# First K transfer in two, two wo transfers in one, and one head's softmax earlier, in a cached-attention decode block

## The chip, the core and the metric

The kernel runs on one NeuronCore of one Trainium2 chip. The core has a matrix engine (PE, whose weight loads are shown as PEld), a vector engine (DVE), a scalar engine (ACT), a general engine (POOL), and a queue of its own, SyncE (SP), which here does nothing but issue transfers from HBM into the on-chip memory, SBUF. Sixteen DMA engines carry these transfers out. The metric is the device time of one execution in microseconds. The median of three runs of the kernel before is 355.0 us (354.94 to 355.05).

## The reference

One token passes through a decoder block. Cut to what matters:

```
mod = silu(c) @ w_mod                     -> six vectors of 512: sa, ca, ga, sb, cb, gb
h   = layernorm(x) * (1 + ca) + sa        x: 1 x 512
q   = h @ wq                              32 heads of 128
for each of 8 KV heads g (4 query heads share one):
    s = q_g . k_cache[g] / sqrt(128)      32768 positions x 128
    p = softmax(s);   o_g = p @ v_cache[g]
x   = x + ga * (concat(o) @ wo)           wo: 4096 x 512
h   = layernorm(x) * (1 + cb) + sb
x   = x + gb * (relu(h @ w1) @ w2)        w1: 512 x 1792, w2: 1792 x 512
```

All inputs are bf16. The two caches are 64 MB each; everything else adds some 13 MB. Every byte is read once, so the block moves 149.42 MB from HBM for very little arithmetic per byte.

## The kernel before, in words

**The stream.** All large inputs come through one list, `stream` (L139 to L144), whose entries are issued in order on the SP queue by `load` and `stream_dma`. A K or V entry is half a head: two "steps" of 64 cache rows per partition, 32 KB on each of the 128 partitions, 4 MB in all. The order is: first half of head 0's K, `w_mod`, `wq`, second half of head 0's K; then, for g from 0 to 6 and for each half, K of head g+1 and V of head g; then V of head 7 (one transfer of two steps, two of one step); then `wo` in four parts, which belong to heads 0 to 3, 4 and 5, 6, and 7 (`WOP`, L47); then `w1` in two parts and `w2` in six. Towards the end of the list the parts get smaller: the two last `wo` parts are 512 KB, the eight `w1` and `w2` parts 1344 to 128 KB.

**Slots and semaphores.** The destinations are five slots of 32 KB per partition (the pool `ring`), used in turn; several small parts share one slot (`piece`). SP can issue an entry only when the compute that read the slot's previous content has finished. The framework also gives the transfers eight completion semaphores in turn, so SP waits until the transfer eight places earlier has landed. When an entry can be issued, it queues behind the entries before it.

**The heads.** For each head, DVE first transposes a quarter of K in place (`turn_k`, L413, four 2.28 us instructions per half head), PE multiplies it with the queries (`scores`, L429), DVE copies the scores of a half head and takes their maximum (`bank_max`, L435). `softmax(g)` (L440) is a Python generator in six pieces, which are emitted one at a time between other work by `next(soft)`: the maximum over the halves (DVE, `m_p`); its transpose (PE, `mT_ps`); the maximum over rows and its spread (DVE, `Mrow`, `Mexp`); the transpose back and the exponential (PE `Mb_ps`, ACT `nbias`, `P_g`); the transpose of the probabilities and the row sums (DVE `PT_g`, `Lexp`); the sum over partitions (PE, `L_ps`); and, when the generator ends, its reciprocal (DVE, `Linv`). `pv(g, (u, u'))` (L484) multiplies the probabilities with half a V: for most heads a loop of the PE's own sequencer (L499), whose entry waits for what the loop needs; for the last stretch it is unrolled.

**The order.** The order of PE and DVE instructions is the one written in the main loop (L606 to L693, `manual_schedule`). Iteration g does the scores of head h = g+1 and, between them, the rest of head g's softmax, the sums of head g-1 (`blocks`, `o_cols`, `normalise`), and both V halves of head g.

**The tail.** After the last V, PE works through a fixed list: `project(0)` to `project(3)` multiply the heads' outputs with the four parts of `wo` (L568 for the first two, L574 for the last two, 16 matmuls with 16 weight loads each), with `join_rows` (L591) between them and a few matmuls without use (`keep_clock`, L604) that keep PE busy. Then come the residual and the second layernorm (L698 to L714, DVE, ACT and two short PE steps), the `w1` product (L721, 16 matmuls, 12 of which need the first `w1` part and the last 4 the second), a transpose and relu (L731, L732), the `w2` product (L742, 56 matmuls, 16 + 12 + 12 + 8 + 4 + 4 for the six parts), two DVE steps (L747, L749) and the store of the result.

Of the kernel before, what the change touches and what calls it, by code (L numbers as in the profile page):

```python
# [17 lines left out]
def kernel(  # L18
# [15 lines left out]
    P = 128  # L34
    _, _, D = A_x.shape
    _, Hkv, Sk, Dh = A_k_cache.shape
    Hq = A_wq.shape[1] // Dh
    REP = Hq // Hkv
# [4 lines left out]
    TK = 64  # L43
# [2 lines left out]

    WOP = [(0, Hkv // 2), (Hkv // 2, Hkv // 4), (Hkv - 2, 1), (Hkv - 1, 1)]  # L47
    WOROWS = 2
    LAST = Hkv - 1
    LOOPED = Hkv - 2  # L50
    W2P = [(0, 4), (4, 7), (7, 10), (10, 12), (12, 13), (13, 14)]
# [9 lines left out]
    vv = A_v_cache[0].rearrange("g (p j) d -> g p j d", p=P)  # L61
    wm_v = w_mod.rearrange("(p kt) n -> p kt n", p=P)
    wq_v = A_wq.rearrange("(p kt) n -> p kt n", p=P)
    def wo_v(i):
        g0, n = WOP[i]
        return A_wo[g0 * REP * Dh:(g0 + n) * REP * Dh, :].rearrange("(p r) d -> p r d", p=P)

    w1_v = B_w1.rearrange("(p kt) f -> p kt f", p=P)
    w2_v = B_w2.rearrange("(p f) d -> p f d", p=P)

# [15 lines left out]
    loaded, last_loop = {}, []  # L86
# [3 lines left out]
    def piece(name, at, n):  # L90

        if name not in pieces:
            pieces[name] = ring.tile([P, 2 * TK * Dh], BF16, tag="slot", name=name)
        return pieces[name][:, at:at + n]

    def load(key):
        kind = key[0]
        if kind == "wm":
            t = ring.tile([P, KT, 6 * D], BF16, tag="slot", name="wm_sb")
            src = wm_v  # L100
        elif kind == "wq":
            t = ring.tile([P, KT, Hq * Dh], BF16, tag="slot", name="wq_sb")
            src = wq_v
        elif kind in "kv":
            g, steps = key[1], key[2]
            src = (kv if kind == "k" else vv)[g, :, TK * steps[0]:TK * (steps[-1] + 1), :]
            name = "Ksb" if kind == "k" else "Vsb"
            if len(steps) == 2:
                t = ring.tile([P, TK * len(steps), Dh], BF16, tag="slot", name=name)
            else:  # L110
                t = piece(name, TK * Dh * (steps[0] % 2), TK * Dh).rearrange("p (j d) -> p j d", d=Dh)
        elif kind == "wo":
            g0, n = WOP[key[1]]
            t = piece("wo_sb", g0 * REP * D, n * REP * D).rearrange("p (r d) -> p r d", d=D)
            src = wo_v(key[1])
        elif kind == "w1":
            k0, k1 = W1P[key[1]]
            t = piece("w12_sb", k0 * Dff, (k1 - k0) * Dff).rearrange("p (kt f) -> p kt f", f=Dff)
            src = w1_v[:, k0:k1]
        else:  # L120
            f0, f1 = W2P[key[1]]
            t = piece("w12_sb", KT * Dff + f0 * D, (f1 - f0) * D).rearrange("p (f d) -> p f d", d=D)
            src = w2_v[:, f0:f1]
        stream_dma(t[:], src)
        if kind in "kv":
            for i, u in enumerate(steps):
                loaded[(kind, g, u)] = t[:, TK * i:TK * (i + 1), :]
        else:
            loaded[key] = t[:]

    def stream_dma(dst, src):
        i = nc.sync.dma_start(out=dst, in_=src)
        tc.stamp_issue_order_token(i.ins, "sp_stream")
        if last_loop:

            tc.add_manual_dep(i.ins, last_loop[0], mybir.DependencyInfo(
                mybir.DependencyClass.NoSync, mybir.DependencyReason.DATA))

    stream = [("k", 0, (0, 1)), ("wm",), ("wq",)] + [("k", 0, (2 * G, 2 * G + 1)) for G in range(1, NG)]  # L139
    for g in range(LAST):  # L140
        for G in range(NG):
            stream += [(kind, gg, (2 * G, 2 * G + 1)) for kind, gg in (("k", g + 1), ("v", g))]
    stream += [("v", LAST, (0, 1)), ("v", LAST, (2,)), ("v", LAST, (3,))] + [("wo", i) for i in range(len(WOP))]
    stream += [("w1", i) for i in range(len(W1P))] + [("w2", i) for i in range(len(W2P))]  # L144
    pos = [0]

# [22 lines left out]
    for hp in range(4):  # L169
        h, par = hp // 2, hp % 2  # L170
# [213 lines left out]
    def build_qbd(g):  # L384
        d_ap = qbd[g % 2][:]
        d_ps = d_ap.ap[0][0]
        s_ap = qrep_sb[:]
        s_ps = s_ap.ap[0][0]
        for a in range(4):
            o = AP(d_ap.tensor, d_ap.offset + (32 * a) * d_ps + 4 * 7 + 32 * a,  # L390
                   [[d_ps, 32], [QW, 4], [1, 4]])
            i = AP(s_ap.tensor, s_ap.offset + (32 * a) * s_ps + REP * g,
                   [[s_ps, 32], [Hq, 4], [1, 4]])
            nc.scalar.copy(out=o, in_=i)  # L394
# [8 lines left out]
    def turn_k(g, u, half):  # L403

        if u == 0 and half == 0:
            S_tiles[g] = spool.tile([P, NG, 512], F32, tag="S_g", name="S_g")
            m_tiles[g] = spool.tile([P, NG], F32, tag="m2", name="m2")
        Ksb = need(("k", g, u))
        KTt = Ksb[:, 32 * half:32 * half + 32, :].rearrange("p j d -> p (j d)")
        KT_tiles[g, u, half] = KTt  # L410
        if g == 0 and u < 2:
            return
        t = nc.vector.transpose(out=KTt.bitcast(F32), in_=KTt.bitcast(F32))  # L413
        if loop:

            tc.add_manual_dep(t.ins, loop.pop(), mybir.DependencyInfo(
                mybir.DependencyClass.NoSync, mybir.DependencyReason.DATA))
# [188 lines left out]
    with tc.manual_schedule(engines={mybir.EngineType.PE, mybir.EngineType.DVE}):  # L606
# [7 lines left out]
        soft = softmax(0)  # L614
# [2 lines left out]
        soft = None  # L617
        for g in range(LAST):
            h = g + 1
            build_qbd(h)  # L620
            turn_k(h, 0, 0)
            turn_k(h, 0, 1)
            turn_k(h, 1, 0)
            scores(h, 0, 0)
            if soft:
                next(soft)
            open_o(g)
            scores(h, 0, 1)
            if soft:
                next(soft)  # L630
            if g > 0:
                blocks(g - 1)
            scores(h, 1, 0)
            if g > 0:
                o_cols(g - 1)
            turn_k(h, 1, 1)
            scores(h, 1, 1)
            if soft:
                next(soft)
            if g > 0:  # L640
                normalise(g - 1)
                if g in [sum(w) for w in WOP]:
                    spread(part_of(g - 1))
            if soft:
                next(soft)
            bank_max(h, 0)
            next(soft or iter(()), None)
            pv(g, (0, 1))
            for u in (2, 3):
                for half in range(2):  # L650
                    turn_k(h, u, half)
                    scores(h, u, half)
            bank_max(h, 1)
            soft = softmax(h)
            next(soft)
            if g < LOOPED:
                pv(g, (2, 3))
                next(soft)
                continue
            next(soft)  # L660
            next(soft)
            pv(g, (2,), range(6))
            next(soft)
            next(soft)
            open_o(LAST)
            pv(g, (2,), range(6, 16))
            pv(g, (3,))
            next(soft)
            next(soft, None)
            a_rows.append(row_bank("a_ps"))  # L670
            blocks(g)
# [109 lines left out]
```

## Time and profile before

| | |
|---|---|
| median of three runs | 355.0 us |
| profiled execution, its own time | 355.01 us |
| its span, first to last instruction | 353.2 us |
| bytes read from HBM, mean rate over the span | 149.42 MB, 423 GB/s |
| share of the 16 DMA engines, SP's queue | 98.5% |
| PE busy | 281.2 us (80%), 1311 matmuls |
| DVE busy | 202.7 us (57%) |
| ACT busy, POOL busy | 25.5 us (7%), 3.9 us (1%) |
| mean granted PE clock | 0.951 |

The span is 1.8 us shorter than the execution's own time; what lies around it is start and end of the program. A share of a busy engine is an average over the whole span and says little about one stretch of it. A group's row gives the line and engine, the operation, what it writes and reads, the count, busy time and mean of one instruction, and then the idle time of that engine right before them and what ended it. The row of a transfer gives the queue, the count, the size, and the median time from issue to landing, which includes the time spent behind earlier transfers.

### The profile page before, as it was taken

The page shows a single profiled execution, that of the slowest core. Times are in us where ns is not written, and L with a number is a line of the kernel's source. Part 1 is how long each engine was busy: PE and PEld are TensorE (multiplying, and loading weights), DVE is VectorE, ACT ScalarE, POOL GpSimd, SP SyncE. Part 2 cuts the span into 40 slices and gives each one's busy share as a digit, 9 for nine tenths or more (in the row PEclk, how much of TensorE's full clock was granted, in tenths as well). Part 3 has the DMA queues.
Part 4 walks back from the last instruction along what each step waited for, and adds up shares of the span by engine and source line. Part 5 has one row for each costly group of instructions (what it writes and reads, how often), then busy time and mean ns, then how long its engine had stood idle before and what let it go on. Part 6 is the DMA issues. An engine that isn't in the chain of part 4 may idle for free. (4 is left out here: it accounts for less than half of the span.)

```text
span 353.2 us, 4005 instructions
## 1 busy us (share of the span) xinstructions
PE 281.2 (80%) x1311; PEld 112.2 (32%) x1311; DVE 202.7 (57%) x271; ACT 25.5 (7%) x69; POOL 3.9 (1%) x16
## 2 busy tenths in 40 slices
PE   0064865499798979897989799979689797989996
PEld 0021322133233333333333333323234233334444
DVE  6672074867458745872769177553938095743141
ACT  1200103000001000100010001000100000011000
POOL 4000000000000000000000000000000000000000
PEclk9995689589999999999999999999969999999999
DMA  8999999999999999999999999999999999999995
GB/s 356 405 426 449 437 416 438 449 419 419 455 430 416 449 442 416 417 460 427 419 453 432 416 442 439 428 414 449 442 416 445 438 423 417 453 434 410 424 419 203
DMA packets 6852, 149.59 MB, mean 423 GB/s; under 512 B 824, under 2 KB 1080, under 8 KB 1976
## 3 DMA queue, kind: packets, MB, share of 16 engines
q1 hardware_dynamic: 6776, 149.43, 98.5%
q8 instruction: 8, 0.13, 0.1%
q14 instruction: 4, 0.03, 0.0%
q0 software_dynamic: 64, 0.00, 0.0%
HBM read 149.42 MB, written 0.00 MB: 423 GB/s over the span
## 5 line engine op out<-in xcount | busy, mean ns | idle before, releaser
L413 DVE STREAM_TRANSPOSE Ksb<-Ksb 128x2048 f32<-128x2048 f32 x60 | 133.9, 2280 | 37.7 <-DMA Ksb<-in_A_k_cache_dram 37.7
L491 PE MATMUL o_ps<-Vsb,PT_g 128*16 (+1 forms) x512 | 128.1, 383 | 21.9 <-issue 9.9
L429 PE MATMUL S_ps<-Ksb,qbd 128*128 128x512 bf16 x512 | 124.0, 395 | 12.4 <-DVE Ksb L413 9.6
L429 PEld LDWEIGHTS <-qbd 128*128 128x128 bf16 x512 | 49.4, 99 | 78.1 <-issue 22.1
L491 PEld LDWEIGHTS o_ps<-Vsb,PT_g 128*16 x416 | 36.1, 87 | 90.2 <-issue 65.9
L435 DVE TENSOR_SCALAR_CACHE_REDUCE S_g<-S_ps 128x512 f32<-128x512 f32 x16 | 11.0, 690 | 52.9 <-PE S_ps L429 52.9
L394 ACT COPY qbd<-qrep_sb 32x16 bf16<-32x16 bf16 x32 | 6.4, 201 | 130.3 <-PE S_ps L429 129.2
L472 DVE STREAM_TRANSPOSE PT_g<-P_g 128x1024 bf16<-128x1024 bf16 x8 | 9.8, 1224 | 7.0 <-ACT P_g L466 7.0
L491 PEld LDWEIGHTS <-PT_g 128*16 128x16 bf16 x96 | 8.2, 90 | 11.0
L463 ACT ACTIVATE nbias<-Mb_ps 128x1 f32<-128x1 f32 x8 | 1.4, 171 | 133.4 <-PE Mb_ps L461 133.4
L295 PE MATMUL mod_ps<-wm_sb,siluT 128*1 128x512 bf16 x24 | 3.6, 624 | 7.4 <-DMA wm_sb<-in_w_mod_dram 7.4
L466 ACT ACTIVATE P_g<-S_g,nbias 128x1024 bf16<-128x1024 f32 x8 | 9.2, 1148 | 0.2
L227 PE MATMUL xc_ps<-cx_sel,cx_bd 16*128 16x2 bf16 x4 | 0.3, 172 | 11.2 <-DVE cx_bd L221 11.2
L358 DVE STREAM_TRANSPOSE Ksb<-Ksb 128x2048 f32<-128x2048 f32 x4 | 8.9, 2282 | 0.0
L522 DVE SCALAR_TENSOR_TENSOR Y<-o_ps,smask,Y 16x128 f32<-16x128 f32 x24 | 8.1, 339 | 0.8
L450 DVE TENSOR_REDUCE Mrow<-mT_ps 1x4 f32<-1x128 f32 x8 | 2.1, 263 | 9.8 <-PE mT_ps L447 9.8
L478 PE MATMUL L_ps<-Lexp,ones_f 128*128 128x4 f32 x16 | 2.9, 254 | 4.3 <-DVE Lexp L475 4.3
L367 PE MATMUL q_ps<-wq_sb,hT 128*1 128x512 bf16 x32 | 3.6, 627 | 3.2 <-DMA wq_sb<-in_A_wq_dram 3.2
L604 PE MATMUL spare_ps<-qbd,ident_bf 128*128 128x512 bf16 x19 | 5.6, 380 | 0.0
L447 PE MATMUL mT_ps<-ident_f,m_p 128*1 128x128 f32 x8 | 2.2, 270 | 3.9 <-DVE m_p L444 2.0
L478 PEld LDWEIGHTS L_ps<-Lexp,ones_f 128*128 128x128 f32 x16 | 3.2, 222 | 5.8 <-issue 5.1
L374 DVE STREAM_TRANSPOSE q_cols<-q_ps 128x512 f32<-128x512 f32 x2 | 1.3, 694 | 5.6 <-PE q_ps L367 5.6
(116 smaller groups left out, 82.1 us busy)
## 6 DMA issues: line engine op xcount, KB each, us to landing
Ksb<-in_A_k_cache_dram SPq DMA_DIRECT2D x16, 4096.0 KB, 31.6
Vsb<-in_A_v_cache_dram SPq DMA_DIRECT2D x15, 4096.0 KB, 32.2
wq_sb<-in_A_wq_dram SPq DMA_DIRECT2D x1, 4096.0 KB, 28.0
Vsb<-in_A_v_cache_dram SPq DMA_DIRECT2D x2, 2048.0 KB, 32.6
wm_sb<-in_w_mod_dram SPq DMA_DIRECT2D x1, 3072.0 KB, 18.8
wo_sb<-in_A_wo_dram SPq DMA_DIRECT2D x1, 2048.0 KB, 30.8
w_sb<-in_B_w_dram SPq DMA_DIRECT2D x1, 1344.0 KB
wo_sb<-in_A_wo_dram SPq DMA_DIRECT2D x1, 1024.0 KB, 32.9
```

Of the source, the lines that this page charges most:

```text
L295: nc.tensor.matmul(dst[j // 4][32 * (j % 4):32 * (j % 4) + 1, :], lhsT=src_T[:, kt:kt + 1], rhs=w[:, kt, j * 512:(j + 1) * 512], start=(kt ...
L358: nc.vector.transpose(out=t, in_=t)
L394: nc.scalar.copy(out=o, in_=i)
L413: t = nc.vector.transpose(out=KTt.bitcast(F32), in_=KTt.bitcast(F32))
L429: nc.tensor.matmul(S_ps_tiles[g], lhsT=qbd[g % 2][:, hp, 4 * (7 - s):4 * (7 - s) + P], rhs=KTv[:, 16 * sl:16 * sl + 16, h, :, par], start= ...
L435: nc.vector.tensor_scalar(out=S_tiles[g][:, G, :], in0=S_ps_tiles[g], scalar1=1.0, scalar2=None, op0=ALU.mult, op1=ALU.max, accum_out=m_ti ...
L466: nc.scalar.activation(out=P_g[:], in_=S_g[:].rearrange("p g f -> p (g f)"), func=ACT.Exp, bias=nbias[:], scale=scale, accum_out=l_g[:],)
L472: nc.vector.transpose(out=PT_g[:], in_=P_g[:])
L478: nc.tensor.matmul(L_ps[:], lhsT=ones_f[:], rhs=Lexp[:], start=True, stop=True)
L491: nc.tensor.matmul(o_tiles[g][:], lhsT=PT, rhs=Vx, start=False, stop=False, skip_group_check=True)
L522: nc.vector.scalar_tensor_tensor(out=Y[:], in0=o[:, s], scalar=smask[:, s:s + 1], in1=Y[:], op0=ALU.mult, op1=ALU.add,)
L604: nc.tensor.matmul(spare[0], lhsT=ident_bf[:], rhs=qbd[0][:, :, 0:P], start=True, stop=True)
```

## The change

Three edits are made together.

1. The first entry of the stream, the first half of head 0's K (32 KB of each partition), is issued as two transfers: the first 16 rows, 4 KB of each partition (512 KB in all), then the other 112 rows, 28 KB of each partition (3584 KB).
2. The last two parts of `wo`, 512 KB each, come as one transfer of 1 MB, which fills the same place in the slot with the same bytes. `project(2)` and `project(3)` keep their order and their matmuls; each now has this one transfer to wait for.
3. In iteration g = 5, five of the pieces of head 6's softmax are emitted ahead of the loop `pv(5, (2, 3))`, where before there was only the first. In iteration g = 6 the generator is finished at once: `turn_k(7, 1, 1)` moves ahead of `scores(7, 0, 0)`, the reciprocal follows it, and all four `scores` of the half head come before `o_cols(5)`.

On the engines this means the following. SP issues two transfers at the start instead of one, and three `wo` transfers instead of four; the total count stays. On PE, `mT_ps` and `Mb_ps` of head 6 stand before that V loop and not among head 7's scores, and `L_ps` stands right behind the loop. On DVE, `Mrow` and `Mexp` stand before the loop, and `PT_g` and `Lexp` before head 7's first K transposes, which were between these steps. The number of matmuls and of DVE operations is the same.

```diff
+    FIRST = 16
...
-    def wo_v(i):
-        g0, n = WOP[i]
-        return A_wo[g0 * REP * Dh:(g0 + n) * REP * Dh, :].rearrange("(p r) d -> p r d", p=P)
...
         elif kind == "wo":
-            g0, n = WOP[key[1]]
-            t = piece("wo_sb", g0 * REP * D, n * REP * D).rearrange("p (r d) -> p r d", d=D)
-            src = wo_v(key[1])
+            parts = key[1]
+            (g0, n), m = WOP[parts[0]], len(parts)
+            t = piece("wo_sb", g0 * REP * D, m * n * REP * D).rearrange("p (g x) -> p g x", g=m)
+            src = A_wo[g0 * REP * Dh:(g0 + m * n) * REP * Dh, :].rearrange("(g p r) d -> p g (r d)", g=m, p=P)
...
-        stream_dma(t[:], src)
+        if key == ("k", 0, (0, 1)):
+            for j0, j1 in ((0, FIRST), (FIRST, 2 * TK)):
+                stream_dma(t[:, j0:j1], src[:, j0:j1])
+        else:
+            stream_dma(t[:], src)
         if kind in "kv":
             for i, u in enumerate(steps):
                 loaded[(kind, g, u)] = t[:, TK * i:TK * (i + 1), :]
+        elif kind == "wo":
+            for m, i in enumerate(parts):
+                loaded[("wo", i)] = t[:, m].rearrange("p (r d) -> p r d", d=D)
...
-    stream += [("v", LAST, (0, 1)), ("v", LAST, (2,)), ("v", LAST, (3,))] + [("wo", i) for i in range(len(WOP))]
+    stream += [("v", LAST, (0, 1)), ("v", LAST, (2,)), ("v", LAST, (3,))] + [("wo", parts) for parts in ((0,), (1,), (2, 3))]
...
             h = g + 1
+            ahead = h == LAST
             build_qbd(h)
             turn_k(h, 0, 0)
             turn_k(h, 0, 1)
             turn_k(h, 1, 0)
+            if ahead:
+                turn_k(h, 1, 1)
+                next(soft, None)
+                soft = None
             scores(h, 0, 0)
...
             scores(h, 1, 0)
+            if ahead:
+                scores(h, 1, 1)
             if g > 0:
                 o_cols(g - 1)
-            turn_k(h, 1, 1)
-            scores(h, 1, 1)
+            if not ahead:
+                turn_k(h, 1, 1)
+                scores(h, 1, 1)
...
             soft = softmax(h)
             next(soft)
+            if g == LOOPED - 1:
+                for _ in range(4):
+                    next(soft)
             if g < LOOPED:
                 pv(g, (2, 3))
                 next(soft)
```

## The prediction

> **What bounds the kernel now.** I read the page's slices, queues and chain first, then the chain in order of time, then the transfers, the PE timeline of the last 13 us and PE's waits there, and the clock by windows.
>
> ```profile
> DMA  8999999999999999999999999999999999999995
> HBM read 149.42 MB, written 0.00 MB: 423 GB/s over the span
> q1 hardware_dynamic: 6776, 149.43, 98.5%
> ...
> 305.52 30.79 DMA wo_sb<-in_A_wo_dram
> 336.33 12.39 DMA w_sb<-in_B_w_dram
> 348.76 1.74 PE ffn_ps L742 x28
> 350.52 0.29 DVE o_rows L747
> 350.83 0.28 DVE o_bf L749
> ```
>
> The transfers bound it: SP's queue keeps all 16 DMA engines busy from the second microsecond to the end, and PE (80%) fits beside them. The chain ends on wo and w1/w2 transfers; only 2.4 us of compute stand behind the last wait. So a gain needs an earlier stream, and a loss can come in two ways: the stream is later, or the tail of PE falls behind it. How closely the tail follows the stream is read in these lines:
>
> ```profile
> wo_sb<-in_A_wo_dram SPq DMA_DIRECT2D x1, 512.0 KB, 33.6
> DMA to landing us min/median/max: 30.8/33.2/34.4
> ...
> 340.05 0.61 PEld L574 LDWEIGHTS <-wo_sb 128*128 128x128 bf16 x16 [0.33 <-DMA wo_sb<-in_A_wo_dram]
> 341.33 0.79 PEld L574 LDWEIGHTS <-wo_sb 128*128 128x128 bf16 x16
> ...
> 344.73 1.24 PE L721 MATMUL hid_ps<-w_sb,h2T 128*1 128x448 bf16 x16 [0.18 <-DVE x_rows L714]
> 346.95 3.53 PE L742 MATMUL ffn_ps<-w_sb,hid_bd 128*4 128x128 bf16 x56 [0.22 <-DMA w_sb<-in_B_w_dram]
> ```
>
> The third wo part is issued at 306.38 and lands 33.6 us later, at 339.98; the fourth is issued at 306.85 and lands 34.4 us later, at 341.25. project(2) begins its weight loads at 340.05 after a wait for that transfer, project(3) at 341.33. Both stand directly behind their transfer, 1.27 us apart.
>
> **The change part by part.**
>
> *The wo parts in one transfer.* The bytes and their place in the stream stay, so the joint transfer lands where the fourth part landed, at 341.25. project(3) sees no difference. project(2) has to wait for the same moment: its first weight load goes from 340.05 to 341.33, +1.28 us. PE runs in order, so behind the waiting instruction stand one keep_clock matmul, join_rows, two more keep_clock matmuls and project(3). In the trace these take 341.33 - 340.05 = 1.28 us from project(2)'s first load to project(3)'s, and nothing in that stretch waits for anything but PE itself. So project(3) ends 1.28 us later, and x1T (L698), the layernorm and h2T follow by the same amount: none of them waits for a transfer.
>
> What of the 1.28 us reaches the end is found from the waits for transfers behind it. First the w1 product: its first 12 matmuls begin at 344.73, in groups of four 0.19 us apart (the next four at 344.92), so the fourth group could begin at 345.30; it begins at 345.61, when the second w1 part (issued 321.74, 23.8 us to landing) is there. That wait hides 0.31 us. Then the w2 product: 56 matmuls at 0.056 us (28 in 1.74 us, of which the last one's own 0.22 us) need 55 x 0.056 + 0.22 = 3.30 us without waits and took 3.53, so 0.23 us more is hidden. The end moves by 1.28 - 0.31 - 0.23 = +0.74 us. The later w2 parts no longer hold PE up: the part that it waited for landed at 336.33 + 12.4 = 348.7, and PE would reach it at about 349.5. One transfer less saves SP one issue of 0.42 us, which is hidden: SP issues these 30 us ahead.
>
> *The first K half in two transfers.* SP issues once more (0.42 us, as the row for the others); this shifts the next four issues, and they all wait behind earlier bytes: wm is issued at 1.20 and its first byte is due only after the 4 MB of K. The stream itself: 512 KB in rows of 4 KB took 1.27 us between the two wo landings; at the 433 GB/s of 4 MB transfers (20.00 to 29.68 us) they take 1.21. Price: +0.06 us. Both other ends come from the start. The first 4 MB land 12.0 us after their issue, and 4 MB at the full rate take 9.7 us; the difference, 2.3 us, is the dead time from the issue at 0.74 to the first bytes in the second microsecond, about 1 us, and some 1.3 us of ramp. If the small transfer removed all the ramp, the stream would be 1.3 us earlier. On the other side, if in each of its 8 rows per engine the small transfer paid such a ramp again, in part, I bound it by the 2.3 us once. The wo rows lie next to each other in HBM and the K rows 64 KB apart, which no 4 KB row of this trace shows. I take +0.06, because the wo row has the same size and number of pieces, and no row shows a ramp that grows with the size of the first transfer.
>
> The Trainium skill, page "DMA: Bandwidth & Descriptors", section "Rules for kernel authors", speaks against this part: it wants at least 1 MiB per transfer, and its section on the anatomy of one DMA gives (for GpSimd's path) a fixed cost of about 2.0 us each, by which the split would cost 2 us and the sum would be 357.8. The two wo landings, 1.27 us apart for 512 KB, show no such cost in a full queue; whether it holds at the head of an empty one no row here shows.
>
> *Head 6's softmax ahead of the V loop.* No instruction is added. From m_p's start to Mexp's end the same steps take 1.06 us for head 7 (314.08 to 315.14), and Mb_ps 0.22 more: PE is ready for the loop at 278.1, not at 276.9. The loop began at 277.79, so it begins 0.3 us later if the loop's entry overlaps these steps, 1.2 us if it follows them. It frees its V slot that much later, for a transfer issued at 286.64 that lands 35.1 us later: three transfers are ahead of it, so this is hidden. In exchange PT_g, Lexp and L_ps are gone from between head 7's scores, and PE no longer waits for the fourth K transpose (1.45 us at 294.3) or for Linv (0.85 us before 297.31): the loop pv(6, (0, 1)) begins about 1.5 us earlier. This gain ends at the next K half:
>
> ```profile
> 302.47 8.89 DVE L413 STREAM_TRANSPOSE Ksb<-Ksb 128x2048 f32<-128x2048 f32 x4 [5.31 <-DMA Ksb<-in_A_k_cache_dram]
> ...
> 305.55 5.58 PE L429 MATMUL S_ps<-Ksb,qbd 128*128 128x512 bf16 x24 [0.19 <-PEq L497]
> 311.42 1.90 PE L429 MATMUL S_ps<-Ksb,qbd 128*128 128x512 bf16 x8 [0.29 <-DVE Ksb L413]
> ```
>
> The half lands at 302.4, DVE needs 8.89 us, and the last eight matmuls already wait for it. PE can start earlier, but not end earlier than 313.3. Even if PE came 1 us late out of this stretch, project(2) now waits 1.28 us anyway. Price: 0, between -0.2 (keep_clock finishing earlier) and +0.3.
>
> Sum against the profiled execution's own 355.01 us (0.01 above the median): 355.01 + 0.74 + 0.06 + 0 = 355.8.
>
> **The rivals.** *The clock falls in the tail.* The granted PE clock fell to half behind a thin window:
>
> ```profile
> 93.08:96.50 3.42, 1.57 (x7) 0.67 (x8) 3.38 (x5) 0.75 (x4) 0.00 (x0) 1.00 1.04 450
> 253.51:256.92 3.41, 1.67 (x9) 0.96 (x9) 3.41 (x4) 0.00 (x0) 0.00 (x0) 1.00 0.96 413
> 256.92:260.34 3.42, 2.14 (x8) 1.13 (x6) 1.03 (x5) 0.00 (x0) 0.00 (x0) 0.50 0.93 403
> 338.84:342.26 3.42, 3.42 (x57) 1.88 (x56) 1.07 (x4) 0.00 (x0) 0.00 (x0) 1.00 1.05 441
> ```
>
> The second column is PE's busy time, the third from the end the clock. 1.67 us busy of 3.41 was followed by half clock; 1.57 once was not. The tail's window has 3.42 and would lose 1.28 us: 2.1, above both, but its project matmuls are short, so it is thinner than it looks. One window at half clock does 1.7 us of work less: 355.8 + 1.7 = 357.5. The page "TensorE: Matmul & The Clock Gate" of the Trainium skill, section "Why this matters for your kernels", puts the limit at an idle gap of about 3 us, by which 1.28 us would be safe and the sum stays 355.8. The trace does not agree: the longest gap in the window before the fall was 1.74 us.
>
> *The split makes the stream start later*, by the 2.3 us above: 355.01 + 0.74 + 2.3 = 358.0. For it: rows 64 KB apart. Against it: the wo row.
>
> *The split lets the stream start earlier, and the kernel gets faster.* Everything in the tail waits for landings, so an earlier stream moves the end one for one. It has to make up 0.74 us before there is a gain, and 1.45 us for one of over 0.2%. The ramp of 1.3 us alone gives 355.01 + 0.74 - 1.3 = 354.5; with 0.3 us of the dead time as well, 354.2. For it: data move at 328, then 197 GB/s in the second and third microsecond. Against it: these are bytes in flight of 32 KB rows, not an idle queue.
>
> *The joint transfer is hidden*, that is, project(2)'s wait is made up by later waits that I read too small: 355.01 + 0.06 = 355.1. Against it: PEld's wait for wo is in the trace.
>
> **How the numbers follow.** 0.2% (0.7 us) is about what a measurement tells from no change. The wait in project(2) alone: 0.55, 355.8, with its own range 355.4 to 356.2, of which 0.35 of 0.55 is over 355.7. Clock falls: 0.17. Later start: 0.06. Hidden: 0.12. Earlier start: 0.10, of which 0.08 passes 0.2%. Slower: 0.35 + 0.17 + 0.06 = 0.58; faster 0.08; the rest, 0.34, within. Below 355.0 lie the 0.10 of the earlier start, above 357.5 about 0.10 (half of the clock's cases, and the later start, up to 358.0): the range is 355.0 to 357.5.
>
> **What will show it.** In the changed kernel, PEld L574's counterpart should wait some 1.3 us for wo, its two groups should stand 1.28 us apart as before, and the w2 product should run 56 matmuls without a wait for a transfer. Head 6's exponential should lie near 278 to 280 us. The first K transfers should land together at about 12.8 us; if at 11.5, the start was the point. A clock of 0.5 after 342 us would show the first rival. The prediction is wrong if the two L574 groups still begin at 340.05, or if the stream's last landing moves by more than 0.3 us.

## The result

The changed kernel takes 355.89 us (median of 13 executions, 355.71 to 357.17) where the kernel before takes 354.98 (13 executions beside them, 354.94 to 355.55). The ratio is 1.0027, with a 95% interval of 1.002 to 1.0035: slower by 0.9 us. The profiled execution's own time is 356.09 us, its span 354.3, against 355.01 and 353.2.

The page of the changed kernel, DMA queues and chain:

```profile
q1 hardware_dynamic: 6904, 149.43, 98.3%
...
HBM read 149.42 MB, written 0.00 MB: 422 GB/s over the span
...
PE 11%; DVE 1%; issue 0%; ACT 0%; ACTq 0%
```

The same bytes come at 422 instead of 423 GB/s, and the chain that ended last no longer has a transfer in it: it runs almost over PE alone, through the last eighth of the span. Where the extra time lies is read from the tail. The changed kernel's PE timeline there (start, duration, then the idle time before and what ended it, where it was over 0.15 us):

```profile
341.97 0.61 PEld L579 LDWEIGHTS <-wo_sb 128*128 128x128 bf16 x16 [0.52 <-DMA wo_sb<-in_A_wo_dram]
...
343.24 0.77 PEld L579 LDWEIGHTS <-wo_sb 128*128 128x128 bf16 x16
...
346.44 0.93 PE L737 MATMUL hid_ps<-w_sb,h2T 128*1 128x448 bf16 x16
348.24 3.29 PE L758 MATMUL ffn_ps<-w_sb,hid_bd 128*4 128x128 bf16 x56
```

project(2) loads its first weights at 341.97, before at 340.05: +1.92 us. The w1 product begins 1.71 later than before (344.73), the w2 product 1.29 later (346.95), and it ends 1.05 later. Neither of the two products waits for a transfer any more: of the 1.92 us, 0.87 went into waits that are gone.

The 1.92 us have two parts. The joint `wo` transfer lands at 341.93; the fourth part landed at 341.28 before, the third at 340.01. So 1.27 us are the wait for the later half, as the change makes it, and 0.65 us come from the stream, which is later everywhere: the first half of head 0's K is complete at 13.54 instead of 12.76, the first `wo` part at 336.93 instead of 336.31, the last `w2` part at 350.64 instead of 350.02. The delay arises in the first microseconds and stays. The transfers that the changed kernel issues there (KB each, us from issue to landing):

```profile
Ksb<-in_A_k_cache_dram SPq DMA_DIRECT2D x1, 3584.0 KB, 12.3
Ksb<-in_A_k_cache_dram SPq DMA_DIRECT2D x1, 512.0 KB, 4.2
```

The 512 KB are issued at 0.74, the 3584 KB at 1.20. Windows of one microsecond (the last column is GB/s, the one before it the DMA engines' busy share), kernel before, then the changed one:

```profile
1.00:2.00 1.00, 0.00 (x0) 0.00 (x0) 0.93 (x2) 1.00 (x1) 0.75 (x2) 1.00 1.14 328
2.00:3.00 1.00, 0.00 (x0) 0.00 (x0) 0.00 (x0) 0.02 (x1) 0.99 (x4) 1.00 0.58 197
```

```profile
1.00:2.00 1.00, 0.00 (x0) 0.00 (x0) 0.93 (x2) 1.00 (x1) 0.75 (x2) 1.00 0.21 45
2.00:3.00 1.00, 0.00 (x0) 0.00 (x0) 0.00 (x0) 0.02 (x1) 0.99 (x4) 1.00 0.90 209
```

Packets start at about 1.77 us in both. A window counts a packet, with all its bytes and all its time, where it starts: in the first of these windows 10 packets of 32 KB start before the change, and 11 of 4 KB after it. So 328 and 45 GB/s are no rates, and the ends of the packets have to be asked. By these, 1 MB is in at 5.10 us before and at 5.78 after, and the 4 MB of the half at 12.43 and 13.24. In the changed kernel 32 of the first 128 packets, of 4 KB, take over 0.2 us, the longest 1.1, while the median one of this size takes 0.159. But the kernel before starts slowly too: its first 16 packets, of 32 KB, take 1.77 us (median), where the median of the stream is 1.21. The time of all packets of that half, spread over the sixteen engines, is 10.23 us before and 10.70 after; packets of median duration would make it 9.70 and 9.77. The start costs 0.53 us of the engines' time before the change, then, and 0.93 after it. Why the small packets lose more no record tells.

The third edit shows in the stretch from head 6's softmax to head 7's scores. PE before, then after:

```profile
277.79 8.68 PE L491 MATMUL o_ps<-Vsb,PT_g 128*16 x32 [1.79 <-issue]
...
294.32 1.90 PE L429 MATMUL S_ps<-Ksb,qbd 128*128 128x512 bf16 x8 [1.45 <-DVE Ksb L413]
...
297.31 8.05 PE L491 MATMUL o_ps<-Vsb,PT_g 128*16 x32 [0.85 <-DVE Linv L481]
```

```profile
280.05 8.17 PE L496 MATMUL o_ps<-Vsb,PT_g 128*16 x28 [1.32 <-issue]
288.38 1.02 PE L496 MATMUL o_ps<-Vsb,PT_g 128*16 x4 [0.16 <-issue]
...
289.96 7.12 PE L434 MATMUL S_ps<-Ksb,qbd 128*128 128x512 bf16 x32
...
299.66 8.08 PE L496 MATMUL o_ps<-Vsb,PT_g 128*16 x32 [1.57 <-DVE S_g L440]
```

The loop `pv(5, (2, 3))` begins 2.26 us later, of which 0.6 are the stream's. Before, its entry (1.79 us without a visible wait) ran beside DVE's `m_p`; now `m_p`, its transpose, `Mexp` and `Mb_ps` come first, up to 278.73, and the entry's 1.32 us behind them. The 32 scores of head 7 then run in one piece, as the edit wants, but the loop `pv(6, (0, 1))` begins 2.35 us later all the same. `o_cols` and what hangs on it (PE waits 0.52 us for `oA` of `normalise`) now stand behind all the scores, and 1.57 us lie before the loop. The row puts these down to `S_g` (`bank_max`), but most of them are the entry itself: PE's sequencer goes through seven waiting steps and a branch, from 298.22 to 299.38, and only one step is held, for 0.25 us, until `bank_max` is done at 298.89. Before, the same steps ran from 296.11 to 297.02, partly beside the last matmuls, and none was held; `Linv`, which the row names, ended at 297.16, when the entry had already gone on (297.08).

The granted clock also falls behind the thinner stretch that the edit leaves ahead of the loop (windows of the changed kernel; PE busy is the second column, the clock the third from the end):

```profile
277.83:281.24 3.41, 1.35 (x7) 0.55 (x6) 1.49 (x3) 1.41 (x3) 0.00 (x0) 1.00 0.89 384
281.24:284.65 3.41, 3.41 (x9) 1.12 (x10) 1.29 (x3) 0.00 (x0) 0.00 (x0) 0.50 1.05 452
```

It falls there in all four profiles of kernels with this edit (half clock from between 278.25 and 281.24), and in one of the ten without it (the split alone, from 278.00). The price can't be read: the loop takes 9.35 us here, 9.32 at full clock in the kernel with split and joint transfer, and 8.68 before.

PE gets back 0.66 us of its lateness at the next K half, and no more. Its last keep_clock matmul ahead of project(2) ends at about 341.94 (before, at 340.22); the joint transfer lands at 341.93. That is why the chain shows PE, though the transfer would have held it just as long.

### The profile page after: what moved, and what is told of

Same layout as the page of the kernel before. It is cut to its first block, busy times and chain, and to the rows that moved or that the text cites. A ratio compares the mean times of both kernels' runs of the same rounds, so it can differ in the third digit from the quotient of the medians.

```text
span 354.3 us, 4009 instructions
## 1 busy us (share of the span) xinstructions
PE 281.7 (80%) x1311; PEld 112.4 (32%) x1311; DVE 203.1 (57%) x271; ACT 25.5 (7%) x69; POOL 3.9 (1%) x16
## 5 line engine op out<-in xcount | busy, mean ns | idle before, releaser
L496 PE MATMUL o_ps<-Vsb,PT_g 128*16 (+1 forms) x512 | 129.6, 391 | 21.3 <-ACT qbd L399 9.0
L496 PEld LDWEIGHTS o_ps<-Vsb,PT_g 128*16 x416 | 36.9, 89 | 90.0 <-issue 64.5
L546 DVE TENSOR_TENSOR oT_sb<-acc_ps,Linv 128x4 bf16<-128x4 f32 x8 | 1.2, 155 | 8.6 <-PE acc_ps L533 8.6
```

The source lines that it names most:

```text
L496: nc.tensor.matmul(o_tiles[g][:], lhsT=PT, rhs=Vx, start=False, stop=False, skip_group_check=True)
```

## The experiments

Times are medians, in us; beside each stands the median of the kernel before, from runs taken along with it. Numbers of landings, and of what stands behind the store's issue, are from one profiled execution each.

### One part at a time

**The split alone.**

```diff
-        stream_dma(t[:], src)
+        if key == ("k", 0, (0, 1)):
+            for j0, j1 in ((0, 16), (16, 128)):
+                stream_dma(t[:, j0:j1], src[:, j0:j1])
+        else:
+            stream_dma(t[:], src)
```

> Only the first K half is split, 4 KB and 28 KB of each partition; wo and the softmax are as before. Theory (the small first transfer makes the whole stream later, and the tail follows the landings one for one): in the changed kernel's trace the wo and w landings are 0.6 us later than before, so this run is 0.6 us slower than before, ratio about 1.0017, with the first 4 MB of K landed at about 13.5 us and not at 12.8. Rival (the prediction's price of the split, 0.06 us, holds, and the later stream comes from the other edits): 0.1 us or less, landing at 12.8.

Measured: 355.93 (355.64 to 356.22) beside 355.12; ratio 1.0021 (1.0012 to 1.003). The first half is complete at 13.30, the last `w2` part lands at 350.50, 0.48 later than before. But the time grew by 0.81. The profiled execution, 0.91 above before's, shows two things besides the stream: 2.39 us instead of 2.04 from the store's issue to SP's last instruction (+0.35), and a fall of the clock at 295 us, which brings the store 0.08 later still. Both are followed up below.

**The joint transfer alone** (the `wo` lines of the diff of the change, nothing else).

> Only the two last wo parts are joined. Theory: project(2) begins 1.28 us later; of this 0.31 us is hidden by the wait for the second w1 part and 0.23 us in the w2 product, as predicted, and 0.3 us more by the waits for the first w1 and the first w2 part, which the prediction left out: +0.4 us, ratio 1.0012. The prediction's own sum: +0.74 us, ratio 1.0021. Rival (hidden): 0.

Measured: 355.54 (355.29 to 356.36) beside 355.12; ratio 1.0012 (1.0003 to 1.002). PE in its tail:

```profile
341.38 0.69 PE L578 MATMUL acc_ps<-o_sb,wo_sb 128*128 128x1 bf16 x16 [1.04 <-DMA wo_sb<-in_A_wo_dram]
...
345.84 0.93 PE L725 MATMUL hid_ps<-w_sb,h2T 128*1 128x448 bf16 x16
...
347.64 3.29 PE L746 MATMUL ffn_ps<-w_sb,hid_bd 128*4 128x128 bf16 x56
```

Against 340.06, 344.73 and 346.95 before, the lateness is 1.32, then 1.11, then 0.69, and the store is issued 0.46 later (351.59 for 351.13). Of 1.32 us, 0.86 are hidden, at four places: 0.21 before the w1 product begins, 0.31 within it, 0.11 before the w2 product begins and 0.23 within that.

**Head 6's softmax ahead alone** (the main loop's lines of the change's diff, nothing else).

> Only head 6's softmax is moved. The prediction: the loop over the first V half of head 6 begins 1.5 us earlier, and the time stays, between -0.2 and +0.3 us. Theory after the changed kernel's trace: the V loop of head 5 begins 1.7 us later, the next one 1.7 us later too, PE comes out of head 7's scores about 1.1 us later, and as nothing makes the wo transfers late here, PE is what the tail waits for: 1.1 us less the hidden 0.85, +0.3 us, ratio 1.0008.

Measured: 355.36 (354.89 to 356.43) beside 355.12; ratio 1.0007 (0.9998 to 1.0016): no difference that the measurement tells from none, though the interval leaves room for 0.6 us. In the profiled execution 1.58 us lie before the loop `pv(6, (0, 1))` here too. But `pv(5, (2, 3))` begins only 0.30 us later than before (278.09), not 1.7, since PE is done with the scores ahead of it 1.4 us earlier (274.62 for 276.01): the clock did not fall near 257 us, as it did in the kernel before (half from 256.92 to 263.75). PE ends head 7's scores 0.57 us later than before (313.89), where 1.1 were expected; the store is issued at 351.19, 0.06 later than before.

**Joint transfer and softmax, no split.**

> Both the joint wo transfer and the moved softmax, without the split. Theory: project(2) begins when both PE and the transfer are there, so the two costs do not add up; the larger one stays, +0.4 us, ratio 1.0012. Rival: they add up, 0.7 us or more. The difference to the whole change, 0.9 us, is then the split's.

Measured: 355.58 (355.25 to 357.24) beside 355.12; ratio 1.0021 (1.0009 to 1.0033). The median is that of the joint transfer alone; the mean is drawn up by 3 of 12 executions at 357.0 to 357.2. The store of the profiled execution is issued at 351.59, as with the joint transfer alone. PE waits for the joint transfer here too:

```profile
341.36 0.69 PE L575 MATMUL acc_ps<-o_sb,wo_sb 128*128 128x1 bf16 x16 [1.08 <-DMA wo_sb<-in_A_wo_dram]
```

### What of the split costs

The theory after these four kernels (theory A) was that small packets at the head of an empty queue are slow. The other candidates were the second issue as such, and rows 64 KB apart. Each of the next kernels is the one before with the split's lines changed as shown.

```diff
-            for j0, j1 in ((0, 16), (16, 128)):
+            for j0, j1 in ((0, 112), (112, 128)):
```

> The kernel before, with the first K half as 28 KB and then 4 KB of each partition (the order of the two pieces turned round). Theory A: the cost of the split comes from the small packets at the head of an empty queue. Then the 4 KB pieces, which now wait behind 28 KB ones, cost nothing: K's first half lands within 0.1 us of before's 12.76, and the time is 355.1 (355.0 to 355.3). Theory B: the cost comes from issuing twice at the start, or from rows 64 KB apart, wherever the small pieces stand: then the half lands at about 13.3 and the time is 355.6 to 355.9, as with the 4 KB piece first.

Measured: 355.56 (355.42 to 355.88) beside 355.20; ratio 1.0013 (1.0004 to 1.0023).

```diff
-            for j0, j1 in ((0, 16), (16, 128)):
+            for j0, j1 in ((0, 64), (64, 128)):
```

> The kernel before, with the first K half as two equal transfers of 16 KB of each partition. Theory A (small first packets cost, by the time that an engine spends on them before the queue is deep): 16 KB packets are at least four times as long, so most of the cost is gone: K's first half lands at 12.8 to 13.0, time 355.0 to 355.4. Theory B (the second issue costs by itself): lands at about 13.3, time 355.6 to 355.9.

Measured: 355.47 (355.36 to 355.89) beside 355.20; ratio 1.0011 (1.0002 to 1.002).

```diff
-        if key == ("k", 0, (0, 1)):
+        if key == ("k", 3, (0, 1)):
```

> The kernel before, with the split of 4 KB and 28 KB made in the first K half of head 3, in the middle of the stream, where the queue is full; the first half of head 0 stays one transfer. Theory A (only the empty queue makes the small packets dear): every landing behind it within 0.1 us of before, time 355.0 to 355.2. Theory B (4 KB rows that lie 64 KB apart are dear wherever they stand): landings behind it 0.5 us later, time 355.6 to 355.9.

Measured: 355.67 (355.51 to 355.94) beside 355.20; ratio 1.0014 (1.0005 to 1.0023).

Judged by the time, theory A failed in all three: they lose 0.3 to 0.5 us wherever the small piece stands. By the landings it came out better, but not whole. With two pieces of 16 KB the first half is complete at 12.94, as it allowed. With the 28 KB first it is complete at 13.06, 0.30 later than before, where 0.1 was allowed. With the split in head 3 the last landing is 0.26 later, between the 0.1 of theory A and the 0.5 of theory B. Here are the profiled executions so far; "store to end" runs from the store's issue to SP's last instruction:

| kernel | transfers on SP | first K half complete | last `w2` lands | store issued | store to end |
|---|---|---|---|---|---|
| before | 48 | 12.76 | 350.02 | 351.13 | 2.04 |
| softmax ahead alone | 48 | 12.82 | 350.08 | 351.19 | 2.03 |
| joint transfer alone | 47 | 12.87 | 350.10 | 351.59 | 2.11 |
| joint transfer and softmax | 47 | 12.91 | 350.08 | 351.59 | 2.11 |
| 28 KB, then 4 KB | 49 | 13.06 | 350.14 | 351.22 | 2.38 |
| 16 KB, 16 KB | 49 | 12.94 | 350.22 | 351.64 | 2.39 |
| split in head 3 | 49 | 12.77 | 350.28 | 351.68 | 2.38 |
| 4 KB, then 28 KB | 49 | 13.30 | 350.50 | 351.69 | 2.39 |
| changed kernel | 48 | 13.54 | 350.64 | 352.19 | 2.03 |

Only with the 4 KB piece at the very start is the last landing later than 350.3. The other splits, up to 350.28, can't be told by it from the kernels without a split, which scatter from 350.02 to 350.26 (350.26 is that of the last kernel below). The packets themselves tell more. Of the 128 packets of 4 KB in head 3's half, 34 take over 0.2 us, the longest 0.38, and spread over the sixteen engines they take 1.56 us, where 128 of the median 0.159 make 1.27. At the very start it is 27 to 33 of 128 in the three profiles that have them, the longest 1.03 to 1.10, and 1.77 to 2.02 us. Behind the 28 KB piece one packet of 128 takes over 0.2 us, and the sum is 1.28. So a small piece ahead of a long one lost some 0.3 us of the engines' time in a full queue too, and more at the empty one. Whether 4 KB rows that lie next to each other would lose as much at the start was not tried. Most of what the other three splits cost stands in the last column, and that goes with the number of transfers.

### The end of the program

SP's transfers use eight completion semaphores in turn, and at the end of the program SP waits for all of them in a fixed order, in seven steps. With 48 transfers, the store among them, its semaphore is in the last step: in the trace, SP does the other six while the store is under way. With 49 it wraps round to the first: SP stands in that step until the store has landed, and does the other six afterwards, 0.06 us each. A kernel that only adds a transfer tells this from any effect of the split:

```diff
         stream_dma(t[:], src)
+        if key == ("v", 3, (0, 1)):
+            stream_dma(extra[:], A_x[0, 0].rearrange("(i n) -> i n", i=4))
```

> The kernel before with one more transfer of 1 KB in the middle of the stream (behind the first half of head 3's V), into a tile that nothing reads. Theory E (the end sequence): a 45th transfer on SP gives the store of the result the first instead of the last of the eight completion semaphores, and SP, which waits for them one by one at the end, does the other seven waits after the store has landed and not while it is under way: from the store's issue to the end 2.39 us instead of 2.04, so 355.4 to 355.6 beside before's 355.15, with wo and w2 landings within 0.15 us of before's. Rival: what the split kernels lost behind the store comes from the split K half itself; then 355.1 to 355.3 here.

(The expectations, here and further down, miscount by four: with the store it is the 49th transfer, not the 45th.)

Measured: 355.45 (355.20 to 355.80) beside 355.16; ratio 1.0007 (0.9998 to 1.0016), so the time alone would not decide it. The profile does: 2.37 us from the store's issue (351.33) to SP's last instruction. The last `w2` part lands 0.21 later than before, more than the 0.15 expected and within the scatter. SP's wait for the store at the end, before and with the additional transfer (us in total, times, longest):

```profile
SPq L776 <- DMA out_dram<-o_bf: 0.4, 1, 0.4
```

```profile
SPq L779 <- DMA out_dram<-o_bf: 0.9, 1, 0.9
```

Before, the other waits are over when 0.4 us of the store are left; here SP waits from the start, and the rest comes behind. The split in the changed kernel does not pay this, since the joint `wo` transfer brings the count back to 48.

### The parts together

The split and the joint transfer, without the softmax edit:

```diff
-    stream += [...] + [("wo", i) for i in range(len(WOP))]
+    stream += [...] + [("wo", parts) for parts in ((0,), (1,), (2, 3))]
...
+            for j0, j1 in ((0, 16), (16, 128)):
```

> The changed kernel without its third edit: the first K half as 4 KB and 28 KB, and the joint wo transfer. Theory E: the joint transfer takes back the 45th transfer, so the store gets the last semaphore again and 2.04 us stand behind its issue; what is left is the later stream (0.5 to 0.6) and the wait in project(2) (0.43): 355.9 to 356.2. Rival, the parts add: 0.8 for the split alone and 0.4 for the joint transfer alone, 356.3 to 356.4. If it comes out at or above the changed kernel's 355.9, head 6's softmax ahead costs nothing beside the other two.

Measured: 356.02 (355.74 to 357.24) beside 355.16; ratio 1.0023 (1.0014 to 1.0032). That is theory E's value, and not the 356.3 to 356.4 of the sum of the parts. The store is issued at 352.20, in the changed kernel at 352.19. PE at project(2):

```profile
341.96 0.69 PE L582 MATMUL acc_ps<-o_sb,wo_sb 128*128 128x1 bf16 x16 [1.22 <-DMA wo_sb<-in_A_wo_dram]
```

It begins within 0.01 us of the changed kernel's, out of a wait of 1.22 us. So without the softmax edit PE has 1.2 us to spare here; in the changed kernel's profile that reserve is used up, and the end is the same. How much the edit takes differs between executions, though: in the profile of joint transfer and softmax, shown above, 1.08 us were left. There the clock had not fallen near 257 us, as it did in the changed kernel (half from 257.35 to 264.17), and PE came to head 6's softmax 1.9 us earlier than in that kernel, of which 0.6 are the stream's.

**PE's own work moved into the wait.** With the joint transfer, `join_rows` and the keep_clock matmuls between the two projects go ahead of project(2):

```diff
-        keep_clock(2)
-        project(2)
-        keep_clock(1)
+        keep_clock(3)
         join_rows()
         keep_clock(2)
+        project(2)
         project(3)
```

> The kernel before with the joint wo transfer, but with the matmuls that stood between project(2) and project(3) (join_rows and the keep_clock ones) moved ahead of project(2), so that PE does them while it waits. project(3) then follows project(2) at once and ends 0.6 us instead of 1.3 us later than before. Theory H (0.86 us of lateness is hidden by the waits for the first and second w1 part and the first w2 parts): nothing reaches the end, 355.1 to 355.3 (of it 0.06 for the store's semaphore, one place ahead of the last). Rival, the sum of the prediction, by which 0.54 is hidden: 355.2 to 355.4. Rival, every part of a wait reaches the end: 355.7.

Measured: 355.31 (354.95 to 355.83) beside 355.16; ratio 1.0004 (0.9995 to 1.0013): the cost of the joint transfer is gone, within what the measurement can tell. Both projects in its timeline, and the two products behind them:

```profile
341.45 1.20 PE L578 MATMUL acc_ps<-o_sb,wo_sb 128*128 128x1 bf16 x32
...
344.99 1.15 PE L724 MATMUL hid_ps<-w_sb,h2T 128*1 128x448 bf16 x16
...
347.19 3.48 PE L745 MATMUL ffn_ps<-w_sb,hid_bd 128*4 128x128 bf16 x56 [0.29 <-DMA w_sb<-in_B_w_dram]
```

The 32 matmuls end at 342.65, 0.44 us later than before's project(3), which ended at 342.21. 0.44 is less than the later waits can hide, by the 0.86 found above and by the prediction's 0.54 alike, so this kernel does not tell the two apart. The w2 product waits for a transfer again: its start is 0.24 later, with landings that are 0.14 to 0.24 later themselves. It does not beat the kernel before.

### The start, and the clock

**Does the kind of the first rows matter?** `w_mod`, whose rows of 24 KB lie next to each other, ahead of the first K half:

```diff
-    stream = [("k", 0, (0, 1)), ("wm",), ("wq",)] + ...
+    stream = [("wm",), ("k", 0, (0, 1)), ("wq",)] + ...
```

> The kernel before, with w_mod, whose rows of 24 KB lie next to each other, issued ahead of the first K half. It asks whether the start of the stream hangs on the kind of the first rows. If the rows 64 KB apart cost something at the head, the wo and w1, w2 landings come 0.2 to 0.6 us earlier and the time is 354.4 to 354.8; if not, they land as before, and the time is 355.0 (354.9 to 355.3). The K transposes start some 8 us later, which the first head's slack has to cover; where it doesn't, PE comes late into the later heads and no landing shows it.

Measured: 355.30 (355.17 to 355.49) beside 355.20; ratio 1.0002 (0.9993 to 1.0011). The last `w2` part lands at 350.20. So rows 64 KB apart show no cost at the head as long as they are long.

**The clock in the middle.** In this kernel's profiled execution, and in those of three of the splits (16 and 16 KB, head 3, 4 KB first), the granted clock fell to half near 295 us. Windows of the kernel with two 16 KB pieces, on the clock's own borders (PE busy is the second column, the clock the third from the end):

```profile
288.73:292.14 3.41, 2.86 (x14) 1.14 (x13) 3.16 (x8) 1.40 (x3) 0.00 (x0) 1.00 1.01 428
292.14:295.56 3.42, 1.69 (x9) 0.87 (x8) 3.42 (x3) 0.02 (x1) 0.00 (x0) 1.00 0.84 364
295.56:298.97 3.41, 2.75 (x10) 1.29 (x8) 1.34 (x8) 0.00 (x0) 0.00 (x0) 0.50 1.04 452
298.97:302.38 3.41, 3.41 (x9) 1.10 (x8) 0.00 (x0) 0.00 (x0) 0.00 (x0) 0.50 1.07 461
```

The same stretch of the kernel before, whose windows lie 1.1 us earlier against the work, has 1.96 us of PE in its thinnest window and keeps the clock. This scatter belongs to the execution rather than to an edit: that profiled execution took 355.89, while the same kernel's median is 355.47, and the mean clock of the kernel before differs from execution to execution (0.946 to 0.966 in the runs beside the first four kernels). Nor is the busy time of a window a sharp border: behind the 1.69 us here the clock fell, and behind 1.57 us it once stayed whole (the kernel before, 93.08 to 96.50). PE then reaches the tail up to 1.4 us late, and the store comes 0.1 to 0.3 us later than the landings alone would make it (here 1.42 us behind the last landing, before 1.11). The Trainium skill, page "TensorE: Matmul & The Clock Gate", section "What's actually happening", calls the clock's window free-running, that is, not in step with the kernel; these profiles agree.

**The long executions.** If a window over project(2)'s wait caused the 357 us executions, PE work in that wait should end them:

```diff
-        keep_clock(2)
+        keep_clock(6)
         project(2)
```

(in the kernel with the joint transfer and the softmax edit).

> The changed kernel without the split, and with six instead of two keep_clock matmuls ahead of project(2), which fill 0.86 us of its wait. Without them 3 executions of 12 took 357.0 to 357.2 beside a median of 355.58. Theory C: in those the clock fell to half in the tail, because a 3.4 us window happened to lie over project(2)'s wait; then none is above 356.3 here, with a median of 355.4 to 355.7. Rival: the long ones come from elsewhere, and again 2 to 4 of 11 are at about 357.

Measured: 355.88 (355.37 to 356.89) beside 355.16; ratio 1.0022 (1.0012 to 1.0031). Theory C is not borne out: three executions are above 356.3, the highest at 356.89, and the median went up, from 355.58 to 355.88. That fits executions in which PE reaches project(2) late already, for other reasons, and pays for four more matmuls; but no long execution was caught with a profile, so their cause stays open.

## Why the prediction was right, and where it was not

The time, 355.8 forecast and 355.89 measured, and the direction came out. The sizes of two of the three terms did not: that the number fits so closely is luck, as their errors have opposite signs.

**The joint transfer, +0.74: right mechanism, wrong size, about +0.4.** The wait is 1.27 to 1.32 us, as worked out, and nothing between the two projects hides any of it. The error is in what is hidden later. The sum had 0.31 for the second `w1` part and 0.23 within the w2 product; both were measured as such. It left out 0.21 before the w1 product and 0.11 before the w2 product. The first was not to be seen in the row taken: it gave 0.18 us of idle time to DVE's `x_rows`, while the first `w1` part had landed only at 344.60 for a start at 344.73. The second was in the quoted row, as 0.22 us of waiting ahead of the w2 product, and was not counted. The corrected size rests on the tail of the joint transfer alone, where the lateness goes from 1.32 to 0.46; the changed kernel's tail agrees. The wait for `wo` itself shows as 0.52 us in the changed kernel, not as the expected 1.3, because PE came late.

**The split, +0.06: wrong, +0.4 to +0.6.** The three kernels with the 4 KB piece first have their last landing 0.48 to 0.62 later than the profile of before, and 0.22 or more later than any kernel without it; between the means of the two groups lie 0.39 us. The step that failed is the choice of the row: "I take +0.06, because the wo row has the same size and number of pieces". That row comes from a full queue and from rows that lie next to each other; none of its packets took over 0.2 us. Of the split's own, 27 to 33 of 128 did. The upper end, 2.3 us, was kept for this case but was far too wide. By its own test ("if the stream's last landing moves by more than 0.3 us") the prediction's reasons were wrong here, even though its number was right. The rule that was weighed, a fixed cost of about 2.0 us for a transfer (the Trainium skill, "DMA: Bandwidth & Descriptors", section "Anatomy of one DMA"), had the sign of it; what was measured is a quarter of that at the head, and elsewhere no more than the scatter of the landings, about 0.25.

**Head 6's softmax, 0: the price held, a step was wrong.** "The loop pv(6, (0, 1)) begins about 1.5 us earlier" is the step that failed: it begins 2.35 later (1.7 without the stream). The working removed two waits of PE. One, 0.85 us for `Linv`, was none: the row names `Linv`, but the time is that of the loop's entry, which stays. The other, for the fourth K transpose, is gone, but the working did not ask what was late next: `o_cols`, which stood ahead of that wait, and with it `normalise` now come behind all the scores, and the entry behind them. The loop `pv(5, (2, 3))` also began 1.65 later beyond the stream, outside the stated 0.3 to 1.2, because the entry's 1.3 us follow the steps whole. What saved the price was its last sentence, that PE may come 1 us late since project(2) waits anyway: with and without this edit the store is issued at 352.19 and 352.20. It was close: PE came 1.2 us later than without the edit, which is the whole wait. Nor do the medians show that the edit alone costs nothing: their interval reaches from 0 to 0.6 us.

**The sum.** Measured, from profiles: +0.62 from the stream and +0.43 from the joint transfer make the store 1.05 later. The 0.43 is what is left beside the stream; the joint transfer alone has 0.46, with a landing 0.05 later, and 0.42 by the medians, of which 0.07 lie behind the store's issue. Forecast were 0.06 and 0.74. An error of 0.56 and one of 0.31, of opposite signs, left 0.25 in the profiles, and 0.1 in the medians.

**The rivals.** A clock that falls in the tail, while PE still has work there, did not show in any of the profiled executions; the window over project(2)'s wait, put at 2.1 us of PE time, has 2.12 where PE comes to it on time, and kept the full clock:

```profile
338.47:341.88 3.41, 2.12 (x16) 0.65 (x15) 1.44 (x5) 0.00 (x0) 0.00 (x0) 1.00 1.04 431
341.88:345.29 3.41, 3.33 (x50) 2.08 (x50) 0.87 (x8) 0.00 (x0) 0.00 (x0) 1.00 0.99 412
```

(the kernel with split and joint transfer). Whether it falls in the rare executions at 357 is not known. "The split makes the stream start later" was half true: its mechanism came in, at a quarter of its price, beside the likeliest case and not in its place. "The split lets the stream start earlier" and "the joint transfer is hidden" are refuted by the landings and by the joint transfer alone. The 328 and 197 GB/s that were weighed for the earlier start count packets where they start, and are no rates.

## What to carry to other kernels

A price read from a row holds for the state of the queue in that row: the first transfer of this program meets an empty queue, where 4 KB pieces lost more than the row from the full queue said, and is best left long. When a wait is lengthened, sum up every later wait for a transfer on the path, those that a row puts down to another engine too, before saying what reaches the end; work that can be done without the awaited data is best put in front of it. An idle time that a row puts down to a releaser can be the engine's own entry into a loop; compare it with the same entry elsewhere before counting it as a gain. And when a stall is removed, look at what used to run inside it, for that work will stand somewhere else.

## What had not been expected

- The number of transfers changes the end of the program: 2.03 to 2.04 us from the store's issue to SP's last instruction with 48 transfers on the queue, 2.11 with 47, and 2.37 to 2.39 with 49, because the store's completion semaphore changes its place in the order of the last waits. That was most of what three of the splits cost, and it came from no transfer's duration.
- 4 KB packets at the very start: up to 1.1 us for one, against a median of 0.159 in the same kernel. In the middle of the stream, ahead of the 28 KB piece, they took up to 0.38; behind it, one of 128 took over 0.2.
- The clock's 3.4 us windows lie differently against a thin stretch of PE work from profile to profile: 1.69 us busy in one (two 16 KB pieces) and the clock fell, 1.96 in another (the kernel before) and it did not. Moving the softmax ahead made a stretch thin enough that the clock fell behind it in four profiles of four.
